# Attention scores written in permuted query order or in token order: a sliding-window attention and SwiGLU kernel on one core

## Chip, core and metric

The kernel runs on one core of a Trainium2 chip. The metric is device time in microseconds (us), the median of several executions. A matmul engine (TensorE, PE in the profile), a vector engine (VectorE, DVE), an activation engine (ScalarE, ACT), a general engine (GpSimd, POOL) and a queue engine (SyncE, SP) work side by side; sixteen DMA engines move data between device memory and the on-chip memory (SBUF). TensorE writes its results to PSUM only, and VectorE and ScalarE read them from there.

## What is computed

Sliding-window causal attention (8 batches, 8 heads, 576 tokens, head size 64, window 64), then a SwiGLU block on all 4608 tokens. Cut to what matters:

```python
def _attn_ref(q, k, v):
    scores = scale * np.matmul(q, k.transpose(0, 1, 3, 2))   # scale = 1/8
    rel = pos[:, None] - pos[None, :]
    mask = (rel >= 0) & (rel < window)                       # window = 64
    scores = np.where(mask, scores, -1000000000.0)
    ...
    attn = attn / (np.sum(attn, axis=-1, keepdims=True) + 1e-09)
    return np.matmul(attn, v)

def _moe_ref(x, w_gate, w_val, w_out):       # x: [4608, 512]
    g = x @ w_gate                           # [4608, 1536]
    silu = g * (1.0 / (1.0 + np.exp(-g)))
    return silu * (x @ w_val) @ w_out        # [4608, 512], float32
```

## The kernel before

**Tiles.** The 4608 tokens are nine tiles of 512 (`NT` = 9). Tile t = 0 to 6 is the first 512 tokens of batch t, tile 8 those of batch 7. Tile 7 (`LAST`) gathers the last 64 tokens of all eight batches. Tile 0 is turned on TensorE by a path of its own (`TURNED` = 1; functions with `first` in their names); tiles 1 to 8 are what follows.

**Stages of a tile.** For tile t the kernel computes scores, exponentials, sums and products (attention), then the gate and value matmuls with SiLU (`gate_value`, L397), then the output projection (`project`, L434). The loop at L652 interleaves them by hand: scores, sums and products of tile t lie between the output matmuls of tile t-1, and the twelve steps of `gate_value` for tile t follow. The order of the code is the order on each engine's queue; `tc.manual_schedule()` means that nothing reorders it.

**Order of the query columns.** Queries and keys arrive with 16 (queries) or 4 (keys) tokens per partition row, and VectorE turns them in 32x32 blocks. `turn_q` (L194) leaves the queries of a tile in the order (e, r): token 16 r + e of the tile stands at column 32 e + r. `turn_k` (L207) writes the keys in token order, with a step of four elements. `blocks` (L65) picks from a row of 512 such columns the tokens of 64-token blocks lo to hi: for each of 16 values of e, 4 (hi - lo) neighbouring columns.

**Scores** (L244). Each set `(t, w)` covers four heads in four 64x64 quadrants of the array (h and x each 0 or 1). Per block j of 64 keys, four matmuls multiply the keys of the block with the 128 queries of blocks j and j+1 (64 at the end; in tile 7, pieces of 64 throughout). The result goes to `s_ps` at L262: each 64-query block has its 64 columns in the order (e, y), with y = 0 to 3 for the row within the block. For the write order of a matmul (e, then block n, then y) this means runs of four adjacent fp32, the runs 64 columns apart for the two blocks and adjacent again for the next e.

**Exponentials.** Exp (L274) reads the set flat and writes `E` (bf16), a flat product with `mask` (L277) sets the window, and `both` (L282) adds the two key blocks that a query block sees.

**Sums** (`totals`, L291): `both` times ones, per quadrant 512 columns, read as (j, e, y) and written to `d_ps` as (e, j, y), which is again the order of the queries; runs of four. `sums` and `sums_wide` turn them into reciprocals by Ln and Exp. **Products** (`mix`, L336): values times `E`, read as (n, e, y) and written to `ao_ps` through `blocks`, again in runs of four. `scale` (L356) multiplies both into `xT`, whose 512 columns are hence in (e, r) order for tiles 1 to 8.

**Output** (L407 to L453). `project_part` multiplies 128 columns of `hT` at a time with `wo`, so each output row tile `os_` holds 128 rows: four values of e with 32 rows each. `project_end` copies it from PSUM and issues four stores, each of 32 rows that lie 16 token rows apart in the output. All stores are on SP's queue, except for the last tile (t = 8), where every second one is on ACT's. `project_last` (L439) does the last 128 rows in two halves of 256 columns, with four stores each, two on SP's and two on ACT's queue. Loads of values (`stage_v`, L155) are on SP's queue too; loads of queries and keys are on POOL's.

The mask is set up once at L609 to L617: `tri` is copied into `mask` with its columns rearranged to (e, y).

Of the kernel before, what the change touches and what calls it, by code (L numbers as in the profile page):

```python
# [8 lines left out]
P = 128  # L9
FP32 = mybir.dt.float32  # L10
BF16 = mybir.dt.bfloat16
# [6 lines left out]
def kernel(  # L18
# [10 lines left out]
    nc = tc.nc  # L29
    S, D, H = 576, 64, 8  # L30
    NTOK, DFF, DM = 4608, 1536, 512
    NT = NTOK // 512
    TURNED = 1
    LAST = NT - 2

    ctx.enter_context(tc.manual_schedule())
    cst = ctx.enter_context(tc.tile_pool(name="cst", bufs=1))
# [19 lines left out]
    ones = cst.tile([P, 512], BF16, name="ones")  # L57
    tri = cst.tile([P, 2, 64], BF16, name="tri")
    bias = cst.tile([P, 2, 4, 4, 2, 16], BF16, name="bias")
    mask = cst.tile([P, 8, 2, 16, 4], BF16, name="mask")  # L60

    def batch(t):
        return t if t < LAST else t - 1

    def blocks(ap, t, lo, hi):  # L65

        e = 4 if t < TURNED else 16
        w = 64 // e
        return ap.rearrange("r (e x) -> r e x", e=e)[:, :, w * lo:w * hi]

    staged, queries, weights, inverse, xT, hT = {}, {}, {}, {}, {}, {}
# [111 lines left out]
    def transposes(tp, src):  # L183

        for e in range(4):
            nc.tensor.transpose(tp[:, P * e:P * e + P], src[:, e], identb[:])
# [54 lines left out]
    def half(x):  # L241
        return slice(64 * x, 64 * x + 64)

    def scores(t, w):  # L244

        qT = queries[t]
        s_ps = [wide("s_ps") for _ in range(2)]
        for j in range(8):
            if t == LAST:
                k_j = kT[t % 2 if j < 4 else 2]  # L250
                pieces = [(j, j + 1, 0, k_j, P * (j % 4) + 64),
                          (j, j + 1, 1, k_j, P * (j % 4))]
            else:
                pieces = [(j, min(8, j + 2), 0, kT[t % 2], 64 * j)]
            for lo, hi, c, src, k0 in pieces:
                for h in range(2):
                    for x in range(2):
                        slot = s_ps[h][half(x)].rearrange("r a b -> r (a b)")
                        n = hi - lo
                        o = P * j + 64 * c  # L260
                        nc.tensor.matmul(  # L261
                            slot[:, o:o + 64 * n].rearrange(  # L262
                                "r (n e y) -> r e n y", n=n, e=16
                            ),
                            src[half(h), 2 * w + x, k0:k0 + 64],
                            blocks(qT[half(h), 2 * w + x], t, lo, hi).rearrange(
                                "r e (n y) -> r e n y", n=n
                            ),
                        )
        n = 1024 if t == LAST else 960  # L270
        for h in range(2):
            E = eb[2 * w + h]
            flat = E[:].rearrange("r s z -> r (s z)")[:, 64:64 + n]
            nc.scalar.activation(  # L274
                flat, s_ps[h][:].rearrange("r a b -> r (a b)")[:, 0:n], AF.Exp, scale=0.125
            )
            nc.vector.tensor_mul(  # L277
                flat, flat, mask[:].rearrange("r j c e y -> r (j c e y)")[:, 0:n]
            )
            both = epool.tile([P, 8, 64], BF16, name="both", tag="both")  # L280
            lo = 2 if t == LAST else 0
            nc.vector.tensor_add(both[:], E[:, 1:17:2], E[:, lo:lo + 15:2])  # L282
            weights[t, w, h] = E, both
# [7 lines left out]
    def totals(t, w, d):  # L291
        for h in range(2):
            for x in range(2):
                nc.tensor.matmul(  # L294
                    d[x][half(h)].rearrange("r (e j y) -> r j e y", e=16, j=8),
                    ones[half(x), 0:D],
                    weights[t, w, h][1][half(x)].rearrange("r j (e y) -> r j e y", e=16),
                )

    def room(n):  # L300
        return fsb.tile([P, 2, 512], FP32, name="r", tag="r", bufs=4)[:, 0:n]
# [34 lines left out]
    def mix(t, w, o):  # L336
        E = [weights.pop((t, w, h))[0] for h in range(2)]
        for j in range(8) if t == LAST else (0, 2, 4, 6, 1, 3, 5, 7):
            if t == LAST:
                pieces = [(j, j + 1, 2 * j + 1 + c, vl[:, j, 1 - c]) for c in range(2)]  # L340
            else:
                pieces = [(j, min(8, j + 2), 2 * j + 1, vb[t % 2][:, j])]
            for lo, hi, s0, src in pieces:
                n = hi - lo
                for h in range(2):
                    for x in range(2):
                        nc.tensor.matmul(  # L347
                            blocks(o[x][half(h)], t, lo, hi).rearrange(
                                "r e (n y) -> r n e y", n=n
                            ),  # L350
                            src[half(x), w, h],
                            E[h][half(x), s0:s0 + n].rearrange("r n (e y) -> r n e y", e=16),
                            start=lo == 0 and s0 == 1, stop=lo == 7 and (t != LAST or s0 == 16),
                        )

# [9 lines left out]
    def wide(name):  # L365
        return ps_a.tile([P, 2, 512], FP32, name=name, tag="a")
# [48 lines left out]
    def project_end(t, s, o_ps, copy=nc.vector.tensor_copy):  # L415
        os_ = fsb.tile([P, 512], FP32, name="os_", tag="os_", bufs=4)
        copy(os_[:], o_ps[:])
        rows = out[S * batch(t):S * batch(t) + 512]
        if t < TURNED:
            nc.sync.dma_start(rows.rearrange("(r e) f -> e r f", e=4)[s], os_[:])  # L420
            return
        if t == LAST:
            rows = out.rearrange("(b s) f -> b s f", s=S)[:, 512:S]
            rows = rows.rearrange("b (r e) f -> e b r f", e=16)
        else:
            rows = rows.rearrange("(r e) f -> e r f", e=16)
        for i in range(4):
            eng = nc.scalar if t == NT - 1 and i % 2 else nc.sync
            eng.dma_start(rows[4 * s + i], os_[32 * i:32 * i + 32])

    def out_tile():
        return ps_f.tile([P, 512], FP32, name="o_ps", tag="g")
# [4 lines left out]
        project_end(t, s, o_ps)  # L437

    def project_last(t, s):  # L439
        rows = out[S * batch(t):S * batch(t) + 512].rearrange("(r e) f -> e r f", e=16)  # L440
        os_ = fsb.tile([P, 512], FP32, name="os_", tag="os_", bufs=4)
        tiles = out_tile(), out_tile()
        for x in range(2):
            f = slice(256 * x, 256 * x + 256)
            for c in range(12):
                nc.tensor.matmul(  # L446
                    tiles[x][:, 0:256], hT[t][:, c, P * s:P * s + P], wo[:, c, f],
                    start=(c == 0), stop=(c == 11),
                )
            nc.vector.tensor_copy(os_[:, f], tiles[x][:, 0:256])  # L450
            for i in range(4):
                eng = nc.scalar if i % 2 else nc.sync
                eng.dma_start(rows[4 * s + i][:, f], os_[32 * i:32 * i + 32, f])  # L453

    def set_exp():
        nc.scalar.preload_act_table_set("natural_log_exp_and_others")  # L456
# [27 lines left out]
    for a in range(2):  # L484
        tr = tri[64 * a:64 * a + 64]
        nc.gpsimd.affine_select(
            out=tr[:, 1 - a], in_=tr[:, 1 - a], compare_op=ALU.is_ge, fill=0.0,
# [3 lines left out]
            out=tr[:, a], in_=tr[:, a], compare_op=ALU.is_ge, fill=0.0,  # L491
# [24 lines left out]
    def join(copy, dst, src):  # L516
        copy(dst.rearrange("r e (h d) -> r h e d", h=2), src)  # L517
# [52 lines left out]
    d_ps, r = wide("d_ps"), room(2)  # L570
# [33 lines left out]
    for m in range(12):  # L604
        if m < 2:
            gate_end(0, m, pairs[m])
        else:
            gate_value(0, m)
        if m == 2:  # L609
            for x in range(2):  # L610
                for c in range(2):
                    nc.vector.tensor_copy(
                        mask[half(x), 0, c],
                        tri[half(x), x ^ c].rearrange("r (y e) -> r e y", e=16),
                    )
            for i in (1, 2, 4):
                nc.vector.tensor_copy(mask[:, i:2 * i], mask[:, 0:i])  # L617
            for E in eb:
                nc.vector.memset(E[:, 0], 0.0)
        if 5 <= m < 9:  # L620
            u = m - 5
            join(on_a, keys[:, u], raw_k[:, 2 * u:2 * u + 2])
        if 6 <= m < 10:
            u = m - 6
            tp = ps_a.tile([P, 512], BF16, name="tp", tag="a")
            transposes(tp, keys[:, u])
            split_k(kT[1][:, u, :], tp[:])
        if m >= 9:
            turn_q(1, m - 9)
# [92 lines left out]
```

## Time and profile before

| What | Value |
|---|---|
| Median of 3 runs | 328.4 us (328.14 to 328.59) |
| Span of the profiled execution, first to last instruction | 326.2 us |
| Median less span | 2.2 us |
| Mean granted TensorE clock | 0.999 |
| Instructions | 6959 |
| Score matmuls (L261) | 576, 186 to 241 ns |
| Sum matmuls (L294) | 64, 372 to 401 ns |
| Product matmuls (L347) | 576, 186 to 240 ns |
| DMA packets | 82,865, 40.84 MB |

The profile gives one execution's span and no other time of it; so the span stands beside the median of the timed runs, which is longer by 2.2 us. A matmul's duration in the profile is that of a pipelined instruction: four quadrants run together and the next four start before these end, so that the starts tell the rate and the durations overlap. A line number names the line of the kernel that issued the instruction; a group in a view has the same line, engine, operation and tile names. Names like `PE s_ps L261` mean the engine, the tile written and the line. SPq and ACTq are the parts of SP and ACT that issue DMAs.

### The profile page before, as it was taken

What the parts mean: (1) busy time and instruction counts of PE and PEld (TensorE: products, weight loads), DVE (VectorE), ACT (ScalarE), POOL (GpSimd) and SP (SyncE); (2) the same over time, 40 slices, a digit from 0 to 9 for tenths busy, and PEclk for the clock granted to TensorE, in tenths of its full rate; (3) what the DMA queues carried; (4) which work ended last, traced back from release to release, by engine and by line L of the source; (5) the groups of instructions that cost most, each with busy time, mean ns of one, the idle gap of its engine ahead of it and who ended that gap; (6) DMA issues with size and microseconds to landing.
All of it is one profiled execution on the core that took longest, in us unless ns stands there. A gap on an engine that the chain in (4) does not pass through costs nothing.

```text
span 326.2 us, 6959 instructions
## 1 busy us (share of the span) xinstructions
PE 315.9 (97%) x2700; PEld 150.7 (46%) x2743; DVE 220.2 (67%) x352; ACT 167.2 (51%) x239; POOL 142.8 (44%) x256
## 2 busy tenths in 40 slices
PE   8899999999999999999999999999999999999995
PEld 3444444444444444444444544454444544444443
DVE  5865755587766776887678766876697586773431
ACT  5855557337733683358336743565347633773300
POOL 5944545986085893586024989464200000000000
PEclk9999999999999999999999999999999999999999
DMA  7999999999789999959812999799401300020013
GB/s 253 200 202 202 206 146 215 170 146 143 164 160 206 138 151 205 192 81 214 175 38 29 169 173 92 53 191 195 97 2 34 99 0 2 16 83 32 2 33 98
DMA packets 82865, 40.84 MB, mean 125 GB/s; under 512 B 64272, under 2 KB 78352, under 8 KB 82832
## 3 DMA queue, kind: packets, MB, share of 16 engines
q0 software_dynamic: 50672, 23.08, 57.7%
q1 hardware_dynamic: 31136, 16.26, 19.3%
q10 hardware_dynamic: 1024, 1.05, 1.1%
q8 instruction: 21, 0.34, 0.4%
q14 instruction: 12, 0.10, 0.1%
HBM read 54.00 MB, written 9.44 MB: 194 GB/s over the span
## 4 chain that ended last, share of the span: by engine, by line
PE 86%; DMA 8%; POOL 3%; issue 1%; DVE 1%; SPq 0%; DVEq 0%; POOLq 0%
PE o_ps L410 28%; PE g_ps L401 26%; PE v_ps L401 25%; DMA wv<-in_moe_w_val_dram 4%; DMA q_s<-in_q_dram 3%; PE s_ps L261 3%; PE ao_ps L347 2%; PE d_ps L294 1%; DMA q_f<-in_q_dram 1%; POOL wg L172 1%; POOL wv L172 1%; PE o_ps L446 1%; POOL v L129 1%; POOL qk_b L517 0%; DVE qT L198 0%
## 5 line engine op out<-in xcount | busy, mean ns | idle before, releaser
L394 ACT ACTIVATE sg<-g_ps 128x512 f32<-128x512 f32 x108 | 64.4, 597 | 113.8 <-PE g_ps L401 85.1
L395 DVE TENSOR_TENSOR hT<-sg,v_ps 128x512 bf16<-128x512 f32 x108 | 74.7, 693 | 59.8 <-PE v_ps L401 49.2
L401 PE MATMUL g_ps<-xT,wg 128*128 128x512 bf16 x415 | 108.2, 379 | 0.9
L401 PE MATMUL v_ps<-xT,wv 128*128 128x512 bf16 x415 | 107.2, 379 | 0.1
L410 PE MATMUL o_ps<-wo,hT 128*128 128x512 bf16 x396 | 93.6, 380 | 1.5 <-issue 0.3
L108 POOL DMA_DIRECT2D k_s<-in_k_dram x112 | 60.6, 552 | 26.2 <-DMA q_s<-in_q_dram 15.3
L401 PEld LDWEIGHTS <-wv 128*128 128x128 bf16 x424 | 41.5, 98 | 50.1
L401 PEld LDWEIGHTS <-wg 128*128 128x128 bf16 x424 | 41.3, 98 | 49.5 <-issue 0.6
L410 PEld LDWEIGHTS <-hT 128*128 128x128 bf16 x420 | 39.1, 98 | 46.5 <-issue 1.8
L274 ACT ACTIVATE eb<-s_ps 128x960 bf16<-128x960 f32 (+1 forms) x32 | 29.5, 974 | 16.4 <-PE s_ps L261 16.3
L208 DVE STREAM_TRANSPOSE kT<-k_s 128x512 bf16<-128x512 bf16 x28 | 36.0, 1284 | 0.3 <-issue 0.3
L277 DVE TENSOR_TENSOR eb<-eb,mask 128x960 bf16<-128x960 bf16 (+1 forms) x32 | 21.1, 658 | 14.4 <-ACT eb L274 14.4
L359 DVE TENSOR_TENSOR xT<-ao_ps,r 128x512 bf16<-128x512 f32 x36 | 23.0, 684 | 6.5 <-PE ao_ps L347 4.8
L162 POOL CAST vb<-v_f 128x512 bf16<-128x512 f32 x20 | 11.4, 618 | 31.9 <-DMA v_f<-in_v_dram 22.1
L304 ACT ACTIVATE r<-d_ps 128x512 f32<-128x512 f32 (+1 forms) x33 | 20.8, 629 | 6.2 <-PE d_ps L294 5.9
L198 DVE STREAM_TRANSPOSE qT<-q_s 128x512 bf16<-128x512 bf16 x32 | 22.4, 702 | 0.8 <-DMA q_s<-in_q_dram 0.8
L307 ACT ACTIVATE r<-r 128x512 f32<-128x512 f32 (+1 forms) x33 | 22.0, 669 | 1.0
L88 POOL DMA_DIRECT2D q_s<-in_q_dram x28 | 15.2, 564 | 10.2 <-DVE qT L198 4.8
L137 POOL DMA_DIRECT2D vb<-in_v_dram x16 | 10.9, 710 | 8.7 <-DMA wo<-in_moe_w_out_dram 3.7
L282 DVE TENSOR_TENSOR both<-eb 128x512 bf16<-128x512 bf16 x32 | 13.6, 425 | 1.1
L456 ACT ACT_TABLE_LOAD x9 | 11.5, 1283 | 2.0 <-issue 1.9
L95 POOL DMA_DIRECT2D q_s<-in_q_dram x16 | 8.6, 629 | 7.4 <-DVE qT L198 7.4
(107 smaller groups left out, 185.2 us busy)
## 6 DMA issues: line engine op xcount, KB each, us to landing
q_s<-in_q_dram POOLq DMA_DIRECT2D x28, 248.0 KB, 6.0
k_s<-in_k_dram POOLq DMA_DIRECT2D x112, 56.0 KB, 4.8
v_f<-in_v_dram SPq DMA_DIRECT2D x40, 128.0 KB
wo<-in_moe_w_out_dram POOLq DMA_DIRECT2D x3, 512.0 KB, 12.3
q_f<-in_q_dram SPq DMA_DIRECT2D x4, 256.0 KB
vb<-in_v_dram POOLq DMA_DIRECT2D x16, 64.0 KB, 2.9
v<-in_v_dram POOLq DMA_DIRECT2D x16, 64.0 KB, 3.1
q_s<-in_q_dram POOLq DMA_DIRECT2D x16, 62.0 KB, 3.6
```

Of the source, the lines that this page charges most:

```text
L108: nc.gpsimd.dma_start(k_s[p0:p0 + 32, g, :, 0:w], k[b, a:H:2, s:s + P].rearrange("u (r e) d -> r u (e d)", e=4) [:, :, 32 * c:32 * c + w],)
L198: nc.vector.transpose(queries[t][:, u, :].rearrange("r (e x) -> r e x", e=16), staged[t][0][:, u].rearrange("r (e d) -> r e d", d=D)[:, :, ...
L208: nc.vector.transpose(dst[:, u, :].rearrange("r (g x e) -> r g e x", g=4, e=4), k_s[:, :, u].rearrange("r g (e d) -> r g e d", d=D)[:, :, ...
L274: nc.scalar.activation(flat, s_ps[h][:].rearrange("r a b -> r (a b)")[:, 0:n], AF.Exp, scale=0.125)
L277: nc.vector.tensor_mul(flat, flat, mask[:].rearrange("r j c e y -> r (j c e y)")[:, 0:n])
L304: nc.scalar.activation(r, d_ps, AF.Ln)
L307: nc.scalar.activation(r, r, AF.Exp, scale=-1.0)
L359: nc.vector.tensor_mul(xT[t][:, u, :], o_ps, inverse.pop((t, u)))
L394: nc.scalar.activation(sg[:], g_ps[:], AF.Silu)
L395: nc.vector.tensor_mul(hT[t][:, m, :], sg[:], v_ps[:])
L401: nc.tensor.matmul(ps[:], w[:, c, P * m:P * m + P], xT[t][:, c, :], start=(c == 0), stop=(c == 3),)
L410: nc.tensor.matmul(o_ps[:], hT[t][:, c, P * s:P * s + P], wo[:, c, :], start=(c == 0), stop=(c == 11),)
```

## The change

For tiles 1 to 8, the scores are written to `s_ps` at (n, y, e) instead of (n, e, y): inside each 64-query block the columns stand in token order 16 y + e. The matmul still walks (e, n, y), so that successive columns of one matmul land 16 fp32 apart. `E`, `both` and `mask` are then in token order, the sums and products read and write contiguous columns without a rearrangement, `xT` is in token order, and 128 columns of it are 128 successive tokens. So each output row tile goes out with one store on SP's queue (two in tile 7, where its rows belong to two batches), also in the last tile, where ACT had every second one. Tile 0 is as it was.

```diff
-    mask = cst.tile([P, 8, 2, 16, 4], BF16, name="mask")
+    mask = cst.tile([P, 8, 2, 64], BF16, name="mask")
...
                             slot[:, o:o + 64 * n].rearrange(
-                                "r (n e y) -> r e n y", n=n, e=16
+                                "r (n y e) -> r e n y", n=n, e=16
                             ),
...
-                    d[x][half(h)].rearrange("r (e j y) -> r j e y", e=16, j=8),
-                    ones[half(x), 0:D],
-                    weights[t, w, h][1][half(x)].rearrange("r j (e y) -> r j e y", e=16),
+                    d[x][half(h)], ones[half(x), 0:D],
+                    weights[t, w, h][1][half(x)].rearrange("r j z -> r (j z)"),
...
-                            blocks(o[x][half(h)], t, lo, hi).rearrange(
-                                "r e (n y) -> r n e y", n=n
-                            ),
+                            o[x][half(h)][:, 64 * lo:64 * hi],
                             src[half(x), w, h],
-                            E[h][half(x), s0:s0 + n].rearrange("r n (e y) -> r n e y", e=16),
+                            E[h][half(x), s0:s0 + n].rearrange("r n z -> r (n z)"),
...
-        if t == LAST:
-            rows = out.rearrange("(b s) f -> b s f", s=S)[:, 512:S]
-            rows = rows.rearrange("b (r e) f -> e b r f", e=16)
+        elif t == LAST:
+            for i in range(2):
+                r0 = S * (2 * s + i) + 512
+                nc.sync.dma_start(out[r0:r0 + 64], os_[64 * i:64 * i + 64])
         else:
-            rows = rows.rearrange("(r e) f -> e r f", e=16)
-        for i in range(4):
-            eng = nc.scalar if t == NT - 1 and i % 2 else nc.sync
-            eng.dma_start(rows[4 * s + i], os_[32 * i:32 * i + 32])
+            nc.sync.dma_start(rows[P * s:P * s + P], os_[:])
...
             nc.vector.tensor_copy(os_[:, f], tiles[x][:, 0:256])
-            for i in range(4):
-                eng = nc.scalar if i % 2 else nc.sync
-                eng.dma_start(rows[4 * s + i][:, f], os_[32 * i:32 * i + 32, f])
+            nc.sync.dma_start(out[r0:r0 + P, f], os_[:, f])
...
-                    nc.vector.tensor_copy(
-                        mask[half(x), 0, c],
-                        tri[half(x), x ^ c].rearrange("r (y e) -> r e y", e=16),
-                    )
+                    nc.vector.tensor_copy(mask[half(x), 0, c], tri[half(x), x ^ c])
```

More of the change, by code (lines that the diff above doesn't have):

```diff
@@ L277, in scores @@
             nc.vector.tensor_mul(
-                flat, flat, mask[:].rearrange("r j c e y -> r (j c e y)")[:, 0:n]
+                flat, flat, mask[:].rearrange("r j c z -> r (j c z)")[:, 0:n]
             )
@@ L420, in project_end @@
             nc.sync.dma_start(rows.rearrange("(r e) f -> e r f", e=4)[s], os_[:])
-            return
-        if t == LAST:
-            rows = out.rearrange("(b s) f -> b s f", s=S)[:, 512:S]
-            rows = rows.rearrange("b (r e) f -> e b r f", e=16)
-        else:
-            rows = rows.rearrange("(r e) f -> e r f", e=16)
-        for i in range(4):
-            eng = nc.scalar if t == NT - 1 and i % 2 else nc.sync
-            eng.dma_start(rows[4 * s + i], os_[32 * i:32 * i + 32])
+        elif t == LAST:
+            for i in range(2):
+                r0 = S * (2 * s + i) + 512
+                nc.sync.dma_start(out[r0:r0 + 64], os_[64 * i:64 * i + 64])
+        else:
+            nc.sync.dma_start(rows[P * s:P * s + P], os_[:])
     def out_tile():
@@ L439, in project_last @@
     def project_last(t, s):
-        rows = out[S * batch(t):S * batch(t) + 512].rearrange("(r e) f -> e r f", e=16)
+        r0 = S * batch(t) + P * s
         os_ = fsb.tile([P, 512], FP32, name="os_", tag="os_", bufs=4)
```

## The prediction

> **What bounds the kernel now.** I read the busy shares, then the chain of work that ended last, then what TensorE waited for. Shares of the span and then of the chain:
>
> ```profile
> PE 315.9 (97%) x2700; PEld 150.7 (46%) x2743; DVE 220.2 (67%) x352; ACT 167.2 (51%) x239; POOL 142.8 (44%) x256
> ...
> PE 86%; DMA 8%; POOL 3%; issue 1%; DVE 1%; SPq 0%; DVEq 0%; POOLq 0%
> ```
>
> All that TensorE waited for, whole kernel (line, releaser, us in total, times, longest):
>
> ```profile
> PE warm L481 <- DVE ones L470: 1.1, 1, 1.1
> PE s_ps L230 <- DVE kT L189: 1.1, 2, 1.0
> PE g_ps L381 <- DVE xT L359: 0.6, 1, 0.6
> ```
>
> TensorE is busy 97% of the span, is 86% of the chain, and its named waits lie in the start-up and the first tile (lines 481, 230, 381), which the change leaves alone. The SP queue has 0% of the chain. So in tiles 1 to 8 a microsecond added to or taken from TensorE's stream moves the end by a microsecond; whatever DVE, ACT, POOL or SP save lies under it. Only the tail, after the last matmul, has another owner. The question is therefore what each matmul form costs with its new output pattern. The forms that the change touches, and two contiguous ones to compare (shape, count, busy us, mean ns of one):
>
> ```profile
> L261 PE MATMUL s_ps<-qT,kT 64*64 64x128 bf16 x392 | 8.5, 218 | 0.3 <-DVE qT L198 0.3
> L347 PE MATMUL ao_ps<-eb,vb 64*64 64x128 bf16 x392 | 6.9, 217 | 0.0
> L294 PE MATMUL d_ps<-both,ones 64*64 64x512 bf16 x64 | 6.6, 390 | 0.0
> ...
> L261 PE MATMUL s_ps<-qT,kT 64*64 64x64 bf16 x184 | 4.2, 192 | 0.0
> ...
> L446 PE MATMUL o_ps<-wo,hT 128*128 128x256 bf16 x24 | 2.8, 273 | 0.0
> ```
>
> The page has the same form with 512 columns, line 410, at 380 ns. A contiguous column thus costs (380 - 273)/256 = 0.418 ns. The scores (L261), which today write PSUM in runs of four fp32, pay (218 - 192)/64 = 0.41 ns. One set of each kind in order of time (start, us of the merged group):
>
> ```profile
> 74.05 0.62 PE L261 MATMUL s_ps<-qT,kT 64*64 64x128 bf16 x32
> 74.60 3.84 PE L410 MATMUL o_ps<-wo,hT 128*128 128x512 bf16 x16
> ...
> 83.34 0.41 PE L294 MATMUL d_ps<-both,ones 64*64 64x512 bf16 x4
> 83.58 1.01 PE L347 MATMUL ao_ps<-eb,vb 64*64 64x128 bf16 x64
> 84.53 2.77 PE L410 MATMUL o_ps<-wo,hT 128*128 128x512 bf16 x11
> ```
>
> From start to next start, a set of scores holds TensorE for 0.55 us. Four 64*64 quadrants run at once, so its 32 matmuls are 7 x 128 + 64 = 960 columns deep: 960 x 0.418 = 0.40 us of streaming and 0.15 us around it. A tile's products hold it for 0.95 us, of which 2 x 960 columns are 0.80; one sum for 0.24 us, of which 512 columns are 0.21. All three already stream at the contiguous price.
>
> **The change, part by part.**
>
> *Sums and products (L294, L347) become contiguous.* Same instructions, same columns. As they pay the contiguous column price already, I take 0. The far end, if all that stands around the columns came from the runs: 16 sums x 0.03 + 8 products x 0.15 = 1.7 us gained. At the other end a contiguous output has no reason to be dearer than the 0.418 of L410, so no loss.
>
> *Scores (L261) scatter each column.* The same 576 matmuls with the same moving operand now write token order: successive columns go 16 fp32 apart in PSUM, no two neighbours adjacent, where today four are. No row of TensorE writes single elements at a stride, so I bound it. Lower end 0: a run of four costs nothing today, and if the write port takes any address at full rate, singles cost nothing either; a gain is excluded because 0.41 ns is already the contiguous price. Upper end, by the nearest rows for single-element scatter, which are VectorE's:
>
> ```profile
> L208 DVE STREAM_TRANSPOSE kT<-k_s 128x512 bf16<-128x512 bf16 x28 | 36.0, 1284 | 0.3 <-issue 0.3
> ...
> L198 DVE STREAM_TRANSPOSE qT<-q_s 128x512 bf16<-128x512 bf16 x32 | 22.4, 702 | 0.8 <-DMA q_s<-in_q_dram 0.8
> ```
>
> Same operation and shape; L198 writes its columns in contiguous runs, L208 at steps of four elements: 1284/702 = 1.83 times as long. That is what a doubling of the streaming part gives with 2 x 702 - 1284 = 120 ns of fixed time beside 582 ns. Another engine and another memory, but the only pair in the trace that differs in this. Column time of all scores: tiles 1 to 6 and 8 have 2 sets x 960 columns, tile 7 2 x 1024, in all 15,488 x 0.418 = 6.5 us. At 1.83 times, +5.4 us; at a full doubling, +6.5. I take +6.2, nearer the doubling, since the columns are pure streaming and the 0.15 us around a set isn't in the 6.5; tile 7's 64-column pieces hide some of theirs. Both ends, 0 and +6.5, stay for the range.
>
> [...]
>
> What is behind a slower score set: exp (L274), the mask product and `both` start 0.4 us later per set. They have 16 or so output matmuls (3.84 us in the view) between the two sets to hide in, and the whole stream shifts with them, so no new wait.
>
> *Mask and exp.* Exp, mask product and `both` read and write the same flat shapes: 0. Four start-up copies of 64x64 (L612, 206 ns each) lose their rearrangement, on DVE under the first tile's matmuls: 0, and were they uncovered, less than their 0.8 us.
>
> *Stores.* Each output row tile of tiles 1 to 8 goes by one DMA (two for tile 7) instead of four. An SP issue takes about 0.42 us (L429), so SP saves some 1.3 us per row tile, but SP is no part of the chain; the bytes and the 2 KB rows are the same. Loads of `v_f` queued behind stores on SP start up to 1.3 us earlier; POOL's casts wait on them, TensorE doesn't. ACT loses ten issues, all after its last activation. Without that cover nothing here turns into a cost.
>
> *The tail* is what shows. Now (SP's and ACT's queues, and DVE):
>
> ```profile
> 321.47 2.09 SPq L453 DMA_DIRECT2D out_dram<-os__4457  x4
> 321.48 2.16 ACTq L453 DMA_DIRECT2D out_dram<-os__4457  x4
> 322.33 0.42 DVE L450 COPY os__4457<-o_ps 128x256 f32<-128x256 f32 x1 [0.89 <-PE o_ps L446]
> ```
>
> The last copy ends at 322.75 and the last of the issues, ACT's second, at 321.48 + 2.16 = 323.64. One SP issue of 128 rows takes 0.35 to 0.40 us (three of tile 0's four at L420) and would end at 323.15, 0.49 earlier. But all 128 rows then go through one queue and start together, so part is given back: ends 0 and -0.5, I take -0.3.
>
> **Sum.** Against the profiled execution's own span: 326.2 + 6.2 - 0.3 = 332.1 us. The median of the runs shown is 328.4, 2.2 us over that span (launch and end lie around it, untouched); carried over: 334.3 us.
>
> **Rivals.**
>
> 1. *Single scattered columns are free.* Then only the tail counts: 328.4 - 0.3 = 328.1 us, between 327.6 and 328.4. For it: runs of four show no trace of a penalty, and four quadrants write at once without one, so the write side isn't visibly at its limit. Against it: the doubling of L208, where the step is likewise a whole slot per element. It decides from a cost of 0.02 ns per column on (0.3 us over 15,488), below which the tail wins.
> 2. *Free, and contiguous sums and products gain too.* Up to 1.7 us on top: 326.2 to 327.6 us. Against it: they already pay 0.41 ns per column.
> 3. *Scatter costs more than a doubling*, say one column in four slots: +19.4 - 0.3, 347.5 us. Nothing in the trace speaks for it but that the step of 64 bytes is larger than L208's 8.
> 4. *The compiler or the array hides half of it* (each quadrant's writes interleave with the others'): +3 - 0.3, 331.1 us.
>
> **How the numbers follow.** Half rate 0.56, rival 4 0.04, rival 3 0.04: slower 0.64. Rival 1 0.30, rival 2 0.06. A measurement of this kernel can tell about 0.2% (0.66 us) from no change. Rival 1 lies within that save for its far end, to which I give 0.03; so faster 0.09, same 0.27, slower 0.64. Half rate alone would lie between 333.4 (1.83 times, tail -0.4) and 335.0 (doubled, no gain in the tail). The range that holds 8 in 10 must take in rival 1 and rival 4 too: 327.6 to 335.2; rivals 2 and 3 are left out.
>
> **What would show it.** Mean of the 64x128 form at L261 about 270 ns against 218, or, as durations of pipelined matmuls may hide it, start to next start of a set of scores 0.95 us against 0.55; L347, L294, L410 unchanged; in the tail one SP issue after the last copy and none on ACT. It is wrong if a set of scores still takes 0.55 us (rival 1), or if the products' 0.95 us shrinks (rival 2), or if a new TensorE wait appears at L294 or L347.

## The result, and the profile after

| | Before | After |
|---|---|---|
| Median | 328.4 us (328.02 to 328.59, 5 runs) | 334.29 us (334.04 to 335.13, 5 runs) |
| Span of the profiled execution | 326.2 us | 332.2 us |
| Mean granted TensorE clock | 0.999 | 1.000 |
| Ratio of the times | | 1.0185, 95% interval 1.0173 to 1.0198 |

The changed kernel is slower by 1.85%. Its busy shares and its chain, as engines:

```profile
PE 324.8 (98%) x2743; PEld 156.2 (47%) x2743; DVE 220.4 (66%) x352; ACT 167.2 (50%) x239; POOL 143.1 (43%) x256
...
PE 87%; DMA 8%; POOL 3%; DVE 1%; issue 0%; SPq 0%; DVEq 0%; POOLq 0%
```

TensorE still sets the end, and is busy some 9 us longer. Part of that is bookkeeping: the trace of before lacks 43 matmul records, this one none (2700 and 2743 in the two lines), so the busy sums can't be subtracted. The forms that the change touches (shape, count, busy us, mean ns):

```profile
L261 PE MATMUL s_ps<-qT,kT 64*64 64x128 bf16 x392 | 13.7, 307 | 0.5 <-DVE qT L198 0.5
L346 PE MATMUL ao_ps<-eb,vb 64*64 64x128 bf16 x392 | 6.9, 217 | 0.0
L294 PE MATMUL d_ps<-both,ones 64*64 64x512 bf16 x64 | 6.8, 400 | 0.0
L261 PE MATMUL s_ps<-qT,kT 64*64 64x64 bf16 x184 | 6.0, 247 | 0.0
```

The scores moved, from 218 to 307 ns and, in the 64x64 form, from 192 to 247. The sums' mean went from 390 to 400 ns. Starts tell the rate better than these durations. The same stretch as before, in order of time:

```profile
75.02 1.01 PE L261 MATMUL s_ps<-qT,kT 64*64 64x128 bf16 x32
75.97 3.84 PE L407 MATMUL o_ps<-wo,hT 128*128 128x512 bf16 x17
...
85.11 0.41 PE L294 MATMUL d_ps<-both,ones 64*64 64x512 bf16 x4
85.35 1.01 PE L346 MATMUL ao_ps<-eb,vb 64*64 64x128 bf16 x64
86.29 1.04 PE L407 MATMUL o_ps<-wo,hT 128*128 128x512 bf16 x4
```

A set of scores holds TensorE from 75.02 to 75.97, 0.95 us where it was 0.55. A sum (0.24) and a tile's products (0.94 to 0.95) are as before. The tail, SP's queue and DVE:

```profile
327.95 1.64 SPq L445 DMA_DIRECT2D out_dram<-os__4368  x2
328.81 0.43 DVE L444 COPY os__4368<-o_ps 128x256 f32<-128x256 f32 x1 [0.88 <-PE o_ps L440]
```

One store per half is left, none on ACT. From the end of the last copy to the end of the span it is 2.99 us, where it was 3.47: the tail is 0.48 us shorter.

### The profile page after: what moved, and what is told of

The parts are those of the page before. It is cut to its first block, busy times and chain, and to the rows that moved or that the text cites. A ratio compares the mean times of both kernels' runs of the same rounds, so it can differ in the third digit from the quotient of the medians.

```text
span 332.2 us, 6879 instructions
## 1 busy us (share of the span) xinstructions
PE 324.8 (98%) x2743; PEld 156.2 (47%) x2743; DVE 220.4 (66%) x352; ACT 167.2 (50%) x239; POOL 143.1 (43%) x256
## 4 chain that ended last, share of the span: by engine, by line
PE 87%; DMA 8%; POOL 3%; DVE 1%; issue 0%; SPq 0%; DVEq 0%; POOLq 0%
PE o_ps L407 28%; PE g_ps L398 25%; PE v_ps L398 25%; PE s_ps L261 5%; DMA wv<-in_moe_w_val_dram 4%; DMA q_s<-in_q_dram 3%; PE ao_ps L346 2%; PE d_ps L294 1%; DMA q_f<-in_q_dram 1%; POOL wg L172 1%; POOL wv L172 1%; PE o_ps L440 1%; POOL v L129 1%; POOL qk_b L509 0%; DVE qT L198 0%
## 5 line engine op out<-in xcount | busy, mean ns | idle before, releaser
L398 PE MATMUL v_ps<-xT,wv 128*128 128x512 bf16 x424 | 108.8, 379 | 0.0
L407 PE MATMUL o_ps<-wo,hT 128*128 128x512 bf16 x420 | 95.2, 380 | 0.0
L198 DVE STREAM_TRANSPOSE qT<-q_s 128x512 bf16<-128x512 bf16 x32 | 22.4, 703 | 1.0 <-DMA q_s<-in_q_dram 1.0
L88 POOL DMA_DIRECT2D q_s<-in_q_dram x28 | 15.2, 563 | 12.8 <-DVE qT L198 6.8
L261 PE MATMUL s_ps<-qT,kT 64*64 64x128 bf16 (+1 forms) x576 | 16.7, 288 | 0.5 <-DVE qT L198 0.5
L261 PEld LDWEIGHTS <-kT 64*64 64x64 bf16 x576 | 13.1, 134 | 7.5 <-issue 6.6
```

Of the source, the lines that this page charges most:

```text
L198: nc.vector.transpose(queries[t][:, u, :].rearrange("r (e x) -> r e x", e=16), staged[t][0][:, u].rearrange("r (e d) -> r e d", d=D)[:, :, ...
L261: nc.tensor.matmul(slot[:, o:o + 64 * n].rearrange("r (n y e) -> r e n y", n=n, e=16), src[half(h), 2 * w + x, k0:k0 + 64], blocks(qT[half ...
L398: nc.tensor.matmul(ps[:], w[:, c, P * m:P * m + P], xT[t][:, c, :], start=(c == 0), stop=(c == 3),)
L407: nc.tensor.matmul(o_ps[:], hT[t][:, c, P * s:P * s + P], wo[:, c, :], start=(c == 0), stop=(c == 11),)
```

## Experiments

Theory A: a matmul column takes two column times when its neighbour in write order isn't adjacent in PSUM, and the change does nothing else to TensorE's stream. Theory B: it is the distance, or the length of the runs. Theory C: the scatter costs more than that, and contiguous sums and products give some of it back.

### The scatter alone, and the rest alone

Each ratio below is to runs of the kernel before that were taken beside the experiment; their medians lie between 328.23 and 328.55 us. `e1_scatter_only` is the kernel before with this edit alone:

```diff
-                                "r (n e y) -> r e n y", n=n, e=16
+                                "r (n y e) -> r e n y", n=n, e=16
```

> Kernel before with only the write order of the scores changed to token order; sums, products, mask and stores stay as they were, so the columns that they read are in another order than they take them for and the output isn't the reference's. Theory A (each scattered column costs two column times, and nothing else in the change touches TensorE): a set of scores holds TensorE for 0.95 us, sums and products as before, the time is 328.4 + 6.5 = 334.9 us. Theory C (the scatter costs more and contiguous sums and products give some back): above 335.5 us, with the sums' 0.24 us and the products' 0.95 us the same as in the kernel before.

Measured: 335.88 us, ratio 1.0228 (1.021 to 1.0246). A set of scores takes 0.95 us, as A says, but the whole is 1 us over A's 334.9 and in C's range. What TensorE waited for shows where, and it isn't the sums' pattern:

```profile
PE d_ps L294 <- DVE both L282: 0.7, 1, 0.7
```

One sum, in tile 3, held TensorE for 1.11 us instead of 0.24, and the products behind it for 1.17 instead of 0.94: together 1.1 us more. DVE in that stretch, and then POOL:

```profile
116.45 0.66 DVE L277 TENSOR_TENSOR eb<-eb,mask 128x960 bf16<-128x960 bf16 x1 [1.87 <-ACT eb L274]
117.15 0.71 DVE L282 TENSOR_TENSOR both<-eb 128x512 bf16<-128x512 bf16 x1
117.78 2.29 DVE L277 TENSOR_TENSOR eb<-eb,mask 128x960 bf16<-128x960 bf16 x1
```

```profile
115.67 2.16 POOL L108 DMA_DIRECT2D k_l<-in_k_dram  x4
117.82 2.72 POOL L162 CAST vb<-v_f 128x512 bf16<-128x512 f32 x4
```

The second mask product takes 2.29 us instead of 0.66, in the very stretch in which POOL casts the values. POOL comes to that cast when the DMA issues ahead of it on its queue are through (`k_l`, until 117.83), not when TensorE is at some point, so a later set of scores slid onto it: from the kernel before to e1 the cast's start goes from 117.19 to 117.82, that of the second mask product from 114.96 to 117.78. In the changed kernel the cast starts at 118.29, 0.5 us later; its mask product takes 1.06 us and no sum waits:

```profile
117.51 1.06 DVE L277 TENSOR_TENSOR eb<-eb,mask 128x960 bf16<-128x960 bf16 x1
```

```profile
118.29 2.62 POOL L162 CAST vb<-v_f 128x512 bf16<-128x512 f32 x4
```

All fourteen traces of this case agree. Of their 448 mask products, the five that overlap such a cast took 1.06 to 2.44 us (one in the changed kernel, in e1 and in e7, two in e4); the other 443 took at most 0.69. But that is an overlap in time, and no run moved the cast alone. It isn't the whole story either: at its usual 0.66 us the changed kernel's product would have ended at 118.17, before the record of the cast begins. The cause of the slow product stays open; its place is certain. So the extra microsecond sits in tile 3 and not in the score matmuls: A stands, C loses its support.

`e2_scores_back` is the changed kernel with the write order put back to runs of four (the diff above, reversed).

> Changed kernel with only the write order of the scores put back to runs of four; its sums, products and stores stay contiguous, so mask and rows stand in another order than the columns and the output isn't the reference's. Theory A: a set of scores back to 0.55 us, and only the tail differs from the kernel before: 328.4 - 0.5 = 327.9 us, ratio 0.9985. Theory C: contiguous sums and products show their gain, 326.3 to 327.4 us.

Measured: 328.13 us, ratio 0.9999 (0.9984 to 1.0013). `e9_four_stores` puts the four stores back as well, so that contiguous sums and products are all that is left.

> As the run with the scores put back, but with the four stores per row tile of the kernel before as well; left of the change are contiguous sums and products and the mask's plain copy. The mask's order isn't that of the columns, so the output isn't the reference's. Theory A: 328.4 us, no difference from the kernel before, and the 0.5 us of the tail are gone. Theory C: at least 0.5 us below 328.4.

Measured: 328.57 us, ratio 0.9999 (0.9989 to 1.001). The stretch of tile 2 in e9:

```profile
83.25 0.41 PE L294 MATMUL d_ps<-both,ones 64*64 64x512 bf16 x4
83.49 1.01 PE L346 MATMUL ao_ps<-eb,vb 64*64 64x128 bf16 x64
84.44 2.76 PE L407 MATMUL o_ps<-wo,hT 128*128 128x512 bf16 x12
```

C is out: with the scores in runs of four the products hold TensorE for 0.94 to 0.95 us and the sums for 0.24 in both kernels, whatever the order in which they write. Between these two runs only the stores differ: from the last copy to the end 2.98 us with one store, 3.53 with four. The medians of the two differ by 0.44 us, as this says, but their ratios to the kernel before don't tell them apart: the runs of the first spread over 2.1 us, those of the second over 1.0. Part of such a spread lies in the start-up. TensorE waited 0.8 us for the first turned queries of tile 1 in the profile of the one and 0.1 in that of the other, which is more than the gain; that this is what varies in the other runs isn't shown.

### What in the scatter costs

`e3_pairs`, changed kernel, runs of two:

```diff
-                                "r (n y e) -> r e n y", n=n, e=16
+                                "r (m e b) -> r e m b", m=2 * n, e=16
...
-                                "r e (n y) -> r e n y", n=n
+                                "r e (m b) -> r e m b", m=2 * n
```

> Changed kernel, but the scores are written in runs of two columns: two adjacent, the next two 32 columns on, and so on; the moving operand is walked in the same order as ever. The order of the columns no longer fits the mask and the rows, so the output isn't the reference's. Theory A in its pair form (full rate as long as each two successive columns are adjacent): a set of scores at 0.55 us, 327.9 us. Theory B (the run length or the step sets the cost: what a run of four hides, a run of two doesn't): a set between 0.65 and 0.95 us, 329.5 to 334.3 us.

Measured: 328.03 us, ratio 0.9987 (0.9975 to 0.9999). In order of time, one set and what follows:

```profile
74.28 0.62 PE L261 MATMUL s_ps<-qT,kT 64*64 64x128 bf16 x32
74.83 3.84 PE L407 MATMUL o_ps<-wo,hT 128*128 128x512 bf16 x17
```

0.55 us: two adjacent columns are enough. All pairs here start at an even column; a pair that starts at an odd one wasn't tried. `e4_step2`, changed kernel, single columns at the smallest step:

```diff
+                        if t == LAST or j < 6:
+                            p0 = 256 * (j // 2) + j % 2 + 128 * c
+                            dst = slot[:, p0:p0 + 128 * n - 1:2].rearrange(
+                                "r (e n y) -> r e n y", n=n, e=16
+                            )
```

> Changed kernel, but the scores of blocks 0 to 5 (and all of tile 7) are written at every second column, the smallest step that leaves no two successive columns adjacent (8 bytes instead of 64); blocks 6 and 7 stay at a step of 16. The order of the columns no longer fits the mask and the rows, so the output isn't the reference's. Theory A (it counts that the neighbour isn't adjacent, not how far away it is): a set at 0.95 us, 334.3 us. Theory B (the distance sets the cost): most of the 0.40 us per set is gone, a set at 0.55 to 0.75 us, 328.5 to 331.5 us.

Measured: 334.74 us, ratio 1.0189 (1.0172 to 1.0206).

```profile
75.29 1.01 PE L270 MATMUL s_ps<-qT,kT 64*64 64x128 bf16 x32
76.24 3.84 PE L414 MATMUL o_ps<-wo,hT 128*128 128x512 bf16 x17
```

0.95 us at a step of 8 bytes, as at 64: between these two the distance doesn't matter, B is out. (Of the 0.4 us over A's 334.3, the trace has 0.35 at the sum and the products of tile 3, where two mask products met the cast as in e1.) `e5_contiguous` (write order `"r (e n y) -> r e n y"`) closes the other side.

> Changed kernel, but the scores are written fully contiguous, in the order in which the matmul walks its columns. The order of the columns no longer fits the mask and the rows, so the output isn't the reference's. Theory A: as with runs of four, a set at 0.55 us, 327.9 us. Theory B (cost falls with run length): below the runs of four, a set under 0.52 us and under 327.5 us.

Measured: 327.72 us, ratio 0.9983 (0.9972 to 0.9993).

```profile
74.65 0.62 PE L261 MATMUL s_ps<-qT,kT 64*64 64x128 bf16 x32
75.20 3.84 PE L407 MATMUL o_ps<-wo,hT 128*128 128x512 bf16 x17
```

A set at 0.55 us: full contiguity gains nothing over runs of two or four. Of the four ways to write a set, in runs of four, in runs of two, in single columns and contiguous (0.55, 0.55, 0.95 and 0.55 us), only the one without adjacent neighbours costs more.

`e8_sums_scatter` puts the scatter into another form, the sums of the kernel before:

```diff
-                    d[x][half(h)].rearrange("r (e j y) -> r j e y", e=16, j=8),
+                    d[x][half(h)].rearrange("r (j y e) -> r j e y", e=16, j=8),
```

> Kernel before, but the sums (512 columns in each of four quadrants) are written at a step of 16 columns, so that the scatter sits in another matmul form. The sums then stand in another order than the products that they divide, so the output isn't the reference's. Theory A: each of the 16 sums holds TensorE for 0.24 + 0.21 = 0.45 us, the others as before, 328.4 + 3.4 = 331.8 us. If the cost were a matter of the score matmuls alone (short matmuls, many weight loads): 0.24 us and 328.4 us.

Measured: 331.62 us, ratio 1.0095 (1.0078 to 1.0112).

```profile
83.70 0.62 PE L294 MATMUL d_ps<-both,ones 64*64 64x512 bf16 x4
84.11 1.05 PE L347 MATMUL ao_ps<-eb,vb 64*64 64x128 bf16 x64
```

The second sum holds TensorE from 83.70 to 84.11, 0.41 us instead of 0.24, and the products behind it 0.99 instead of 0.94. So the price goes with the columns, not with the score matmuls. The predicted 3.4 us was 3.2 in the medians.

### Alone or by sharing

Four quadrants write at once (the 3,840 columns of a set's 32 matmuls, 1.61 us at 0.418 ns, take 0.55), and for each x the two of h = 0 and 1 write into the same partitions. Does the price come from their sharing? `e6_one_row_group` orders the matmuls of the kernel before by h, `e7_one_row_group_scatter` has the scatter too:

```diff
-        for j in range(8):
+        for h, j in [(h, j) for h in range(2) for j in range(8)]:
...
-                for h in range(2):
+                for _ in range(1):
                     for x in range(2):
```

> Kernel before, but each set of scores does all its matmuls of h = 0 before those of h = 1, so that two quadrants run at once instead of four; all else as it was, and the output is complete. It is the base for the next run. Two streams of 960 columns one after the other: a set of scores holds TensorE for 0.55 + 0.40 = 0.95 us, 328.4 + 6.5 = 334.9 us.

> The run before (h = 0 first, then h = 1) with the scores scattered to token order as in the change; sums and products take the columns for the old order, so the output isn't the reference's. If the double cost belongs to each stream of columns by itself: another 0.80 us per set, 1.75 us, 334.9 + 13 = 347.9 us. If it comes from the two row halves sharing the way into the same PSUM partitions, with room for one scattered stream at full rate: no further cost, 0.95 us per set and 334.9 us.

Measured: 332.5 us, ratio 1.0121 (1.0098 to 1.0144), and 341.93 us, 1.0408 (1.0389 to 1.0426). Neither number is the expected one, because the premise was wrong: the halves don't run one after the other. A set takes 0.81 and 1.37 us. The starts of single matmuls in the first set of tile 2 show how. They come in pairs (x = 0 and 1). In e6 the fifth pair starts 0.25 us after the first, in e7 0.42 us; from there on pairs come twice as densely for a while, so the second half seems to begin long before the first is through. At the end of the set, where by this count only the second half is left, the last five pairs start 55 to 59 ns apart in e6 and 105 to 114 ns apart in e7. With one row half at work the scatter thus costs the double as well, so sharing between the halves isn't its cause. This rests on starts alone; which half a record belongs to the trace doesn't say.

### Looking for a version that keeps the tail and not the price

`best` leaves all as before except for tile 8, where VectorE writes `hT` in token order:

```diff
+        if t == NT - 1:
+            nc.vector.tensor_mul(
+                hT[t][:, m, :].rearrange("p (r e) -> p e r", e=16),
+                sg[:].rearrange("p (e r) -> p e r", e=16),
+                v_ps[:].rearrange("p (e r) -> p e r", e=16),
+            )
+            return
```

> Kernel before with scores, sums and products as they were; in tile 8 alone VectorE writes hT in token order (512 columns at a step of 16), so that its output rows are successive tokens and go out with one store per row tile, two for the last. The output is complete. Theory A: the tail gains its 0.5 us and VectorE's scattered write of 0.7 to 1.3 us stays under a period of 1.73 us per step: 327.9 us, ratio 0.9985. If the slower VectorE write delays the output matmuls: 328.4 to 329 us.

Measured: 332.92 us, ratio 1.0134 (1.0116 to 1.0152). The tail is 2.98 us, but the instruction (min, median, max in ns) and what TensorE waited for:

```profile
L396 DVE TENSOR_TENSOR hT<-sg,v_ps x12: 2329/2532/2535, 293.3 to 316.9; 128x512 bf16<-128x512 f32 x12
```

```profile
PE v_ps L408 <- DVE hT L396: 2.5, 9, 0.3
```

2.53 us against 0.69 contiguous. These instructions overlap in the trace: from start to start it is 2.17 us, which is still longer than the 1.73 us of a step. VectorE became the bound of tile 8, and TensorE waited for it in nine of its steps and once more, 0.9 us, ahead of the output matmuls.

`e10_scattered_read` moves the scatter to the read of the moving operand:

```diff
-                                "r (n y e) -> r e n y", n=n, e=16
+                            slot[:, o:o + 64 * n].rearrange("r (y e) -> r y e", e=16),
...
-                                "r e (n y) -> r e n y", n=n
+                            blocks(qT[half(h), 2 * w + x], t, lo, hi).rearrange("r e y -> r y e"),
```

> Changed kernel, but the score matmuls walk the queries in token order: the scatter moves from the PSUM write to the read of the moving operand (single bf16 at a step of 32 columns, 64 bytes), and the write is contiguous. Output complete, one store per row tile. If only the write pays for single elements: a set of scores at 0.55 us, 327.9 us, ratio 0.9985, below both kernels. If the read pays as the write does: a set at 0.95 us and 334.3 us, or more where the read pays more than one extra column time.

Measured: 347.12 us, ratio 1.0577 (1.0563 to 1.0591).

```profile
76.41 1.85 PE L261 MATMUL s_ps<-qT,kT 64*64 64x128 bf16 x32
78.20 3.84 PE L403 MATMUL o_ps<-wo,hT 128*128 128x512 bf16 x17
```

1.79 us for this set, 1.24 more for 960 columns (1.17 to 1.24 in the sets of tiles 2 to 6 and 8): 1.29 ns on top of 0.418, four column times. Single reads at a step of 64 bytes add three times what single writes add (1.17 to 1.24 against 0.40 us per set).

`e11_pairs_step2_read` writes pairs and lets sums and products read them back in token order, two bf16 apart:

```diff
-                    weights[t, w, h][1][half(x)].rearrange("r j z -> r (j z)"),
+                    weights[t, w, h][1][half(x)].rearrange(
+                        "r j (g e b) -> r (j g) b e", g=2, e=16
+                    ),
...
-                            E[h][half(x), s0:s0 + n].rearrange("r n z -> r (n z)"),
+                            E[h][half(x), s0:s0 + n].rearrange(
+                                "r n (g e b) -> r (n g) b e", g=2, e=16
+                            ),
```

> Scores written in runs of two as in the run with pairs; sums and products read those columns back in token order, at a step of two bf16 (4 bytes), and write contiguous; the mask stands in the pairs' order. Output complete, one store per row tile, so it is the change without a scattered write. If a read at a step of 4 bytes is free: sets, sums and products as in the kernel before, only the tail differs, 327.9 us, ratio 0.9985, below both kernels. If the read pays double as soon as columns aren't adjacent: 16 sums x 0.21 + 8 products x 0.80 more, 327.9 + 9.8 = 337.7 us.

Measured: 328.42 us, ratio 1.0002 (0.9988 to 1.0017).

```profile
83.31 0.43 PE L294 MATMUL d_ps<-both,ones 64*64 64x512 bf16 x4
83.57 1.07 PE L349 MATMUL ao_ps<-eb,vb 64*64 64x128 bf16 x64
84.57 2.76 PE L414 MATMUL o_ps<-wo,hT 128*128 128x512 bf16 x11
```

A sum takes 0.26 us and the products 1.00, against 0.24 and 0.94: 16 x 0.02 + 8 x 0.06 = 0.8 us, which eats the tail's 0.5. This is the whole change without its price, and it is no faster than the kernel before. Reads 4 bytes apart thus cost little here (0.02 us on a sum, 0.06 on a tile's products) and the scores' reads 64 bytes apart four column times (e10): even at 4 bytes a strided read isn't quite free, and steps between the two weren't tried.

## Why the prediction was right

**What bounds the kernel: right.** All that TensorE lost shows at the end. The prediction's list of TensorE's waits leaves out four of 0.3 us; one of them, `PE s_ps L261 <- DVE qT L198`, belongs to tile 1 and comes up below. From the first set of tile 2 to that of tile 3 it was 107.94 - 74.05 = 33.89 us and is 34.69, two sets of 0.40 later.

**The scores, +6.2: right, +6.3** (seven tiles of 0.79 and 0.75 for tile 7, from the starts of their first sets and the last matmul). The half rate is what the runs show: single columns add 0.40 us to a set's 960 columns, 0.42 ns each on top of 0.418 (changed kernel, e4), pairs add nothing (e3), and a sum of 512 single columns takes 0.17 us more (e8). The row that carried the size was a poor witness, and that it fitted is in part luck. It was VectorE's, at a step of 8 bytes; at 32 bytes, in another operation, VectorE's scattered write took 3.7 times its contiguous time (`best`), while TensorE's price is the same at 8 and 64 bytes. Another VectorE row would have led to a wrong size.

**Sums and products, 0: right**, by e9, and rival 2 falls with it. **Rival 1** (scatter free) falls by the set's 0.95 us. **Rival 3** (four slots) is no price of the write, and is that of the read in e10. **Rival 4** (half of it hidden by the quadrants) asked for about 0.75 us and falls by the 0.95 too.

**The tail, -0.3: mis-sized, -0.48**, the far end of its bounds. One queue for all 128 rows gave nothing back: 2.98 to 2.99 us from last copy to end in the eight kernels with one store, 3.47 to 3.54 in the six with four.

**The sum.** 6.3 - 0.48, and 0.18 us in which tile 1 began later (TensorE's wait for the first turned queries, 0.3 us before and 0.5 after, which varies and isn't the change's), give the 6.0 us between the two profiled spans, against the forecast 5.9. The median lies 2.1 us over the span, 2.2 before; what fills that time no run shows. That the median agrees with the forecast 334.3 to a hundredth is luck: errors that cancel.

**"No new wait": right for the changed kernel, by luck.** That the whole stream shifts together is untrue of POOL's casts, which follow POOL's own queue. In e1 a mask product of tile 3 ran beside the cast, and TensorE lost 1.1 us there; in e4, with the changed kernel's rate of scores, 0.35 us.

**What would show it.** The set's 0.95 us came as said; the mean duration of 270 ns did not (307). The durations of these overlapping matmuls aren't a measure of their rate: 218 to 307 ns is 1.41 times, 0.55 to 0.95 us a set 1.73 times.

## What to carry to other kernels

When a layout has to be permuted on TensorE's way into PSUM, keep each two successive columns of a matmul adjacent (here always from an even column on); more contiguity than that bought nothing here (0.55 us a set in pairs, in fours and contiguous), and less doubled the time of a column (0.95 us). Before a scatter is moved to another engine or to the read side, look for a row of that very operation and step: it cost four column times on the moving read (1.24 us more on 960 columns, e10) and 3.7 times on VectorE (2.53 us against 0.69, `best`). Of the fewer, larger stores only the last showed in the time, here 0.5 us (from the last copy to the end 3.47 us before, 2.99 after).

## What was not expected of the hardware

- A VectorE mask product of 0.66 us took 2.29 us beside POOL's casts of 128x512 fp32 to bf16 (e1) and 2.44 us in e7; one that met them in part took 1.06 us (changed kernel). VectorE's products and copies that read PSUM kept to at most 0.72 us beside the same casts.
- VectorE's product with a bf16 output at a step of 32 bytes took 2.53 us against 0.69 us, 2.17 us from start to start (`best`).
- A moving operand read in single bf16 64 bytes apart took about 1.7 ns per column, four times 0.418 (e10).
- With all matmuls of one row half ahead of the other's in the code, the second half appears to start before the first is through: 0.26 us into a set in e6, 0.43 in e7.
